# Regrouping the attention matmuls between the halves of a second matrix product

## The chip, the cores and the metric

One core of one Trainium2 chip. The metric is the device time of the whole program in microseconds; most executions agree within 0.3%, so a difference of 2% (5.1 us) counts as faster or slower and anything less as the same class. Differences under 1% were measured in five alternating rounds against the kernel before on the same chip. Every ratio below is the mean time of one kernel's fast runs over that of the other's of the same rounds, so it is not quite the ratio of the medians that stand beside it.

## The reference, cut to what matters

```python
a   = exp(phi - max) / sum(...)                 # softmax over the 576 rows, 32 memory slots
k_m = einsum('bhsm,bhsd->bhmd', a, k)           # 32 x 64 per head
v_m = einsum('bhsm,bhsd->bhmd', a, v)
x   = softmax(q @ k_m.T / 8) @ v_m              # 8 batches, 8 heads, 576 rows, head dim 64
x   = x.transpose(0, 2, 1, 3).reshape(8, 576, 512)
xn  = (x - mean) / sqrt(var + 1e-6) * g_ln
out = x + relu(xn @ w_ch1) @ w_ch2              # 512 -> 2048 -> 512
```

## The kernel before

The kernel folds v and the first weight into W1b (128 x 2048 for each of two groups of heads), so that a batch's first product is `h = W1b^T Eh`, with Eh the normalised attention weights. A batch then has a first product (16 column blocks j, tile h_ps, evicted as relu into rT) and a second one (ch_ps, 16 matmuls for each output tile of 128 rows, done in halves of 8). Two batches hold nine output tiles: even batches do four, odd ones five. Between the halves of batch b's second product TensorE does the attention part of batch b+1:

```python
    def big(shape, dtype, name):                 # three buffers of two PSUM banks
        return psum.tile(shape, dtype, name=name, tag="big", bufs=3)
    def one(shape, dtype, name):                 # two buffers of one bank: ch_ps
        return psum.tile(shape, dtype, name=name, tag="one", bufs=2)
    ...
    for b in range(1, B):
        mm1(b, 0, JC)                            # first product
        ...
        ex[0] += [a_exp(nb), a_qT(nb, 0), a_kv(nb)]      # after half 0 (lambdas, cut)
        ex[1] += [a_tr(nb)]                              # transposes of k and v
        ex[1] += [x_tiles(pr, t1)]                       # attention output, o_ps, and statistics
        ex[2] += [a_sum(nb), a_w1b(nb, 0), a_w1b(nb, 1)] # softmax sums; W1b, two chunks
        ex[3] += [a_sc(nb), a_vb(nb)]                    # scores
        ex[4] += [a_den(nb)]                             # denominators
        ex[6 if odd else 5] += [a_w1b(nb, 2), a_w1b(nb, 3)]
        ex[8 if odd else 6] += [x_tiles(nb // 2, ...)]   # first two tiles of the next batch
        ...
                mm2(pr, t, 8 * half, 8 * (half + 1))     # a finished tile is put out at once
```

In the names below, kv is the product of exp(phi) with k and v, tr the transposes of its result, sc the scores, den the softmax denominators, o the attention output, and vb the masked copy of v that the o matmuls read. The kv, score, W1b and o matmuls use 64-row tiles of the array (`tile_position`); transposes, sums, denominators and both products use all 128 rows. A tile is put out by one VectorE operation, `x = ch_ps * rstd + x`, which frees its ch_ps buffer; rstd comes from VectorE statistics and two small ACT operations, Ln and Exp.

The softmax here doesn't subtract the row's maximum and nothing guards it: scores larger than these inputs give would overflow.

## Time and profile before

| | before |
|---|---|
| median | 257.06 us (256.99 to 257.06, 3 runs) |
| span of the profiled run | 254.5 us |
| busy: TensorE, VectorE, ACT, GpSimd | 95%, 61%, 51%, 20% |
| batch 1 (from 55.31), even, odd, batch 7 | 30.53, 26.20, 30.03, 29.98 us |

The last row is read from the chain of waits, between the starts of the first products; the prediction shows the lines. The profiled execution was timed at 256.29 us, 0.77 under the median.

### The profile page before, as it was taken

What the parts mean: (1) busy time and instruction counts of PE and PEld (TensorE: products, weight loads), DVE (VectorE), ACT (ScalarE), POOL (GpSimd) and SP (SyncE); (2) the same over time, 40 slices, a digit from 0 to 9 for tenths busy, and PEclk for the clock granted to TensorE, in tenths of its full rate; (3) what the DMA queues carried; (4) which work ended last, traced back from release to release, by engine and by line L of the source; (5) the groups of instructions that cost most, each with busy time, mean ns of one, the idle gap of its engine ahead of it and who ended that gap; (6) DMA issues with size and microseconds to landing.
All of it is one profiled execution on the core that took longest, in us unless ns stands there. A gap on an engine that the chain in (4) does not pass through costs nothing.

```text
span 254.5 us, 5778 instructions
## 1 busy us (share of the span) xinstructions
PE 241.0 (95%) x2422; PEld 131.6 (52%) x2453; DVE 155.0 (61%) x306; ACT 129.1 (51%) x219; POOL 51.8 (20%) x87
## 2 busy tenths in 40 slices
PE   7978999899999999999999999999999999999994
PEld 2534555457434665457444664466544764466453
DVE  3346763684486845695486737684568638683431
ACT  3165662668444582648343672558253663565210
POOL 8633330000900009000710018000900022000000
PEclk9999999999999999999999999999999999999999
DMA  7999999999497492988399483969398541130133
GB/s 157 196 207 207 206 255 231 267 183 159 89 208 148 95 213 44 205 174 152 109 173 204 90 195 56 215 140 175 90 202 177 112 76 41 45 78 5 44 82 82
DMA packets 41922, 36.82 MB, mean 145 GB/s; under 512 B 17444, under 2 KB 37160, under 8 KB 41896
## 3 DMA queue, kind: packets, MB, share of 16 engines
q0 software_dynamic: 17248, 19.53, 45.2%
q1 hardware_dynamic: 24488, 16.79, 28.9%
q8 instruction: 19, 0.31, 0.5%
q10 hardware_dynamic: 160, 0.13, 0.2%
q14 instruction: 7, 0.06, 0.1%
HBM read 41.42 MB, written 9.44 MB: 200 GB/s over the span
## 4 chain that ended last, share of the span: by engine, by line
PE 76%; DMA 17%; DVE 3%; issue 2%; ACT 1%; POOL 1%; POOLq 0%
PE ch_ps L438 42%; PE h_ps L374 22%; DMA q_bf<-in_q_dram 7%; DMA w2b<-in_moe_w_ch_dram 6%; DMA kv_bf<-in_k_dram 3%; PE w1b_ps L353 3%; PE o_ps L404 2%; PE kv_ps L205 2%; PE den_ps L327 2%; PE last_ps L450 1%; PE sc_ps L310 1%; DVE bst L416 1%; POOL q_bf L92 1%; DVE w1b L357 1%; ACT x_sb L410 0%
## 5 line engine op out<-in xcount | busy, mean ns | idle before, releaser
L438 PE MATMUL ch_ps<-w2b,rT 128*128 128x512 bf16 x531 | 125.9, 380 | 2.2 <-issue 1.3
L438 PEld LDWEIGHTS <-rT 128*128 128x128 bf16 x560 | 51.3, 98 | 62.3 <-issue 6.7
L374 PE MATMUL h_ps<-Eh,w1b 128*128 128x288 bf16 x512 | 67.1, 285 | 0.7 <-ACT rT L380 0.5
L380 ACT ACTIVATE rT<-h_ps 128x576 bf16<-128x576 f32 x88 | 52.6, 648 | 21.3 <-PE h_ps L374 21.1
L374 PEld LDWEIGHTS <-w1b 128*128 128x128 bf16 x512 | 49.6, 97 | 17.8 <-issue 2.6
L357 DVE SCALAR_TENSOR_TENSOR w1b<-m_sb,rsum,w1b_ps 128x512 bf16<-128x512 f32 x64 | 43.6, 739 | 4.2 <-ACT m_sb L169 2.6
L382 DVE TENSOR_SCALAR rT<-h_ps 128x576 bf16<-128x576 f32 x40 | 30.3, 757 | 24.0 <-PE h_ps L374 23.9
L410 ACT ACTIVATE x_sb<-o_ps 128x1024 f32<-128x1024 f32 (+1 forms) x20 | 18.6, 937 | 37.8 <-PE o_ps L404 36.5
L462 DVE SCALAR_TENSOR_TENSOR x_sb<-ch_ps,rstd,x_sb 128x512 f32<-128x512 f32 x35 | 26.1, 745 | 15.0 <-PE ch_ps L438 14.4
L189 POOL TENSOR_TENSOR es<-e_sb 128x512 f32<-128x512 bf16 x6 | 6.9, 1149 | 137.9 <-ACT e_sb L182 137.9
L416 DVE BATCH_NORM_STATS2 bst<-x_sb 128x6 f32<-128x512 f32 x36 | 24.4, 677 | 8.1 <-ACT x_sb L410 8.1
L339 DVE SCALAR_TENSOR_TENSOR Eh<-E_sb,rs,rden 128x576 bf16<-128x576 bf16 x16 | 12.4, 814 | 14.1 <-ACT rden L338 14.1
L315 ACT ACTIVATE E_sb<-sc_ps,rs 128x640 bf16<-128x640 f32 x16 | 11.9, 790 | 11.6 <-PE sc_ps L310 11.6
L424 ACT ACTIVATE rstd<-mv,eps_sb 128x2 f32<-128x2 f32 (+1 forms) x20 | 5.9, 296 | 20.3 <-DVE mv L417 20.3
L353 PE MATMUL w1b_ps<-w1r,kvT 64*32 64x512 bf16 x256 | 10.8, 383 | 0.8 <-DVE kvT L258 0.4
L227 DVE CAST v<-kv_ps 128x128 bf16<-128x128 f32 x8 | 2.3, 290 | 14.7 <-ACT k L220 13.7
L174 PE MATMUL w_ps<-fill 128*128 128x512 f32 x14 | 9.7, 814 | 1.6 <-DVE fill L119 1.6
L329 ACT ACTIVATE rden<-den_ps 128x576 f32<-128x576 f32 x16 | 9.5, 644 | 2.7 <-PE den_ps L327 2.7
L182 ACT ACTIVATE e_sb<-phi_st 128x1152 bf16<-128x1152 f32 x8 | 9.2, 1151 | 2.7 <-DMA phi_st<-in_phi_dram 2.7
L338 ACT ACTIVATE rden<-rden 128x576 f32<-128x576 f32 x16 | 10.0, 681 | 0.0
L205 PEld LDWEIGHTS <-e_sb 64*32 64x32 bf16 x648 | 6.3, 90 | 5.0 <-ACT e_sb L182 3.0
L92 POOL DMA_DIRECT2D q_bf<-in_q_dram x10 | 7.6, 757 | 4.6 <-DMA w2b<-in_moe_w_ch_dram 1.9
(69 smaller groups left out, 143.6 us busy)
## 6 DMA issues: line engine op xcount, KB each, us to landing
out_dram<-x_sb SPq DMA_DIRECT2D x70, 128.0 KB, 2.5
kv_bf<-in_k_dram POOLq DMA_DIRECT2D x7, 576.0 KB, 7.0
kv_bf<-in_v_dram POOLq DMA_DIRECT2D x7, 576.0 KB, 9.4
phi_st<-in_phi_dram SPq DMA_DIRECT2D x6, 576.0 KB, 4.7
q_bf<-in_q_dram POOLq DMA_DIRECT2D x6, 576.0 KB, 11.9
w1r<-in_moe_w_ch_dram POOLq DMA_DIRECT2D x4, 512.0 KB, 12.9
w2b<-in_moe_w_ch_dram POOLq DMA_DIRECT2D x4, 512.0 KB, 18.9
q_bf<-in_q_dram POOLq DMA_DIRECT2D x4, 288.0 KB, 11.9
```

The costliest lines, as they stand in the source:

```text
L205: nc.tensor.matmul(ps[32 * j:32 * (j + 1), g, 0:D * (sl.stop - sl.start)], e[r:r + TS, c, j, :], kv[r:r + TS, j, sl, D * c:D * (c + 1)], s ...
L315: nc.scalar.activation(out=E_[:, g].rearrange("p (a x) -> p a x", a=2), in_=sc[:, :, 0:HP], func=AF.Exp, scale=s["rs"][:, g:g + 1])
L339: nc.vector.scalar_tensor_tensor(out=Eh[:, g, :], in0=s["E"][:, g, 0:S], scalar=s["rs"][:, g:g + 1], in1=rd[:, g].rearrange("p a x -> p (a ...
L353: nc.tensor.matmul(ps[32 * j:32 * (j + 1), g, :], s["kvT"][r:r + 64, 2, 32 * j:32 * (j + 1)], w1r[r:r + 64, j, fs], start=True, stop=True, ...
L357: nc.vector.scalar_tensor_tensor(out=s["w1b"][:, g, fs], in0=m_sb[:, fs], scalar=s["rsum"][:, g:g + 1], in1=ps[:, g, :], op0=ALU.mult, op1 ...
L374: nc.tensor.matmul(h_ps[:, half, 0:HS], s["w1b"][:, g, P * j:P * (j + 1)], s["Eh"][:, g, HS * half:HS * (half + 1)], start=(g == 0), stop= ...
L380: nc.scalar.activation(out=dst, in_=h_ps[:, :, 0:HS], func=AF.Relu)
L382: nc.vector.tensor_scalar(out=dst, in0=h_ps[:, :, 0:HS], scalar1=0.0, scalar2=None, op0=ALU.max)
L410: nc.scalar.activation(out=x[:, 0:n].rearrange("p i (u y) -> p i u y", u=2), in_=o_ps.rearrange("p u (i y) -> p i u y", i=2)[:, 0:n], func ...
L416: nc.vector.bn_stats(out=stt, in_=x[:, i, :])
L438: nc.tensor.matmul(ch_ps, rT[:, j, P * t:P * (t + 1)], w2b[:, j, :], start=(j == 0), stop=(j == JC - 1))
L462: nc.vector.scalar_tensor_tensor(out=x, in0=ch_ps, scalar=rstd, in1=x, op0=ALU.mult, op1=ALU.add)
```

## The change

Its intent is to give TensorE fewer and longer groups of attention work: sums, kv and four tiles' o_ps in one group; scores with one W1b chunk; three W1b chunks in another. To allow that, exp and the loads move forward into the batch before, statistics are taken apart from `x_tiles`, and the outputs of an even batch's last two tiles (an odd one's last) go inside the next first product. The core of the diff, cuts marked:

```diff
     def a_kv(b):
         ps = big([P, 2, 512], FP32, "kv_ps")
-        kv_mm(b, ps, slice(0, 2))
         if b < 2:
             kv_sum(b, ps)
-            rs_out(b, ps)
-        k_out(b, ps, True)
+        else:
+            for i in range(2):
+                nc.tensor.matmul(ps[:, 0, P:P + 2], st8[b]["es"][:, i, :], ones8, ...)
+        kv_mm(b, ps, slice(0, 2))
+        k_out(b, ps, b < 2)                      # k now copied by VectorE
         v_out(b, ps[:, :, D:2 * D])
+        rs_out(b, ps)
...
-            nc.vector.tensor_tensor(out=vb[:, g], in0=vsl, in1=vmask, op=ALU.mult)
+            eng = nc.vector if b < 2 else nc.gpsimd
+            eng.tensor_tensor(out=vb[:, g], in0=vsl, in1=vmask, op=ALU.mult)
...
+        mm1(b, 0, 4)
+        for f in late[0:1]: f()                  # rstd and an output of the batch before
+        mm1(b, 4, 7)
+        for f in late[1:2]: f()
+        mm1(b, 7, JC)
...
+        half(0); a_kv(nb); x_tiles(pr, t[0:2], False); x_tiles(pr, t[2:4], False)
+        half(1); a_tr(nb); x_stats(pr, t[0]); x_stats(pr, t[1])
+        half(2); a_sc(nb); x_rstd(pr, t[0:2]); a_w1b(nb, 0); mm2_out(pr, t[0])
+        half(3); a_den(nb, finish=False); mm2_out(pr, t[1]); x_stats(pr, t[2])
+        half(4); a_den2(nb)                      # odd: x_tiles(t[4]); even: three W1b chunks
+        half(5); a_exp(nb + 1)                   # odd: mm2_out(pr, t[2])
+        half(6)                                  # odd: three W1b chunks, statistics of t[4]
...                                               # (conditions and the rest cut)
```

More of the change, by code (lines that the diff above doesn't have):

```diff
@@ L179, in a_exp @@
     def a_exp(b):
-        phi_st, kv, q_bf = loaded[b]
+        phi_st, kv, _ = loaded[b]
         e = att.tile([P, NS, 4, M], BF16, name="e_sb")
@@ L183, in a_exp @@
                              in_=phi_st.rearrange("p j (c m) -> p j c m", m=M), func=AF.Exp)
-        st8[b] = {"e": e, "kv": kv, "q": q_bf}
+        st8[b] = {"e": e, "kv": kv}
         if b >= 2:
@@ L236, in a_kv @@
         ps = big([P, 2, 512], FP32, "kv_ps")
-        kv_mm(b, ps, slice(0, 2))
         if b < 2:
             kv_sum(b, ps)
-            rs_out(b, ps)
-        k_out(b, ps, True)
+        else:
+            for i in range(2):
+                nc.tensor.matmul(ps[:, 0, P:P + 2], st8[b]["es"][:, i, :], ones8,
+                                 start=(i == 0), stop=(i == 1))
+        kv_mm(b, ps, slice(0, 2))
+        k_out(b, ps, b < 2)
         v_out(b, ps[:, :, D:2 * D])
+        rs_out(b, ps)
     def a_tr(b, k_part=True, v_part=True):
@@ L263, in a_tr @@
             s["rsum"] = rsum
-    def a_sum(b):
-        ps = big([P, 2, 512], FP32, "sum_ps")
-        for i in range(2):
-            nc.tensor.matmul(ps[:, 0, P:P + 2], st8[b]["es"][:, i, :], ones8,
-                             start=(i == 0), stop=(i == 1))
-        rs_out(b, ps)
     def a_vb(b):
@@ L277, in a_vb @@
             vsl = s["v2"][:, g, :].unsqueeze(1).to_broadcast([P, 4, D])
-            nc.vector.tensor_tensor(out=vb[:, g], in0=vsl, in1=vmask, op=ALU.mult)
+            eng = nc.vector if b < 2 else nc.gpsimd
+            eng.tensor_tensor(out=vb[:, g], in0=vsl, in1=vmask, op=ALU.mult)
         s["vb"] = vb
+    qTs = {}
     def a_qT(b, i):
-        s = st8[b]
+        q_bf = loaded[b][2]
+        if i == 0:
+            qTs[b] = att.tile([P, 4, NP, P], BF16, name="qT")
         if b > 1:
-            if i == 0:
-                s["qT"] = att.tile([P, 4, NP, P], BF16, name="qT")
-                nc.sync.dma_start_transpose(out=s["qT"].rearrange("p j n x -> p (j n) x"),
-                                            in_=s["q"].rearrange("p j n x -> p (j n x)"))
+            nc.sync.dma_start_transpose(out=qTs[b].rearrange("p j n x -> p (j n) x"),
+                                        in_=q_bf.rearrange("p j n x -> p (j n x)"))
             return
-        if i == 0:
-            s["qT"] = att.tile([P, 4, NP, P], BF16, name="qT")
         q_ps = big([P, 2, 1024], BF16, "qT_ps")
@@ L294, in a_qT @@
             for n in range(NP):
-                nc.tensor.transpose(q_ps[:, u, P * n:P * (n + 1)], s["q"][:, 2 * i + u, n, :], ident)
-        dst = s["qT"][:, 2 * i:2 * i + 2].rearrange("p a n x -> p a (n x)")
+                nc.tensor.transpose(q_ps[:, u, P * n:P * (n + 1)], q_bf[:, 2 * i + u, n, :], ident)
+        dst = qTs[b][:, 2 * i:2 * i + 2].rearrange("p a n x -> p a (n x)")
         if i == 0 or b == 1:
@@ L303, in a_sc @@
         s = st8[b]
-        kvT, qT = s["kvT"], s["qT"]
+        kvT, qT = s["kvT"], qTs[b]
         E_ = att.tile([P, 2, 2 * HP], BF16, name="E_sb", bufs=1)
@@ L385, with x_tiles @@
     xs = {}
-    def x_tiles(pr, ts):
+    def x_tiles(pr, ts, stats=True):
         n = len(ts)
@@ L413, in x_tiles, with x_stats @@
         mv = moe.tile([P, 2, 2], FP32, name="mv", bufs=4)
-        for i in range(n):
-            stt = moe.tile([P, 6], FP32, name="bst", bufs=4)
-            nc.vector.bn_stats(out=stt, in_=x[:, i, :])
-            nc.vector.bn_aggr(out=mv[:, i, :], in_=stt)
         for i, t in enumerate(ts):
             xs[(pr, t)] = (x[:, i, :], mv, i, n)
+        if stats:
+            for t in ts:
+                x_stats(pr, t)
+    def x_stats(pr, t):
+        x, mv, i, _ = xs[(pr, t)]
+        stt = moe.tile([P, 6], FP32, name="bst", bufs=4)
+        nc.vector.bn_stats(out=stt, in_=x)
+        nc.vector.bn_aggr(out=mv[:, i, :], in_=stt)
     def x_rstd(pr, ts):
@@ L544 @@
     a_den(1)
+    load(2)
+    a_exp(2)
     mm2(0, 3, 4, 12)
@@ L549 @@
     mm2_out(0, 3)
-    load(2)
+    a_qT(2, 0)
+    late = []
     for b in range(1, B):
-        pr = b // 2
-        mm1(b, 0, JC)
+        pr, nb = b // 2, b + 1
         odd = b % 2
-        tiles = [4, 5, 6, 7, 8] if odd else [0, 1, 2, 3]
-        t1, t2 = tiles[2:4], tiles[4:5]
-        nb = b + 1
-        if b > 1:
-            x_rstd(pr, tiles[0:2])
-        ex = {i: [] for i in range(2 * len(tiles))}
-        if nb < B:
-            ex[0] += [lambda: a_exp(nb), lambda: a_qT(nb, 0), lambda: a_kv(nb)]
-            if nb + 1 < B:
-                ex[0] += [lambda: phis.update({nb + 1: load_phi(nb + 1)})]
-            ex[1] += [lambda: a_tr(nb)]
-        if b == 1:
-            ex[0] += [lambda: x_tiles(0, [4, 5]), lambda: x_rstd(0, [4, 5])]
-        ex[1] += [lambda: x_tiles(pr, t1)]
-        if nb < B:
-            ex[2] += [lambda: a_sum(nb), lambda: a_w1b(nb, 0), lambda: a_w1b(nb, 1)]
-        ex[2] += [lambda: x_rstd(pr, t1)]
-        if nb < B:
-            ex[3] += [lambda: a_sc(nb)]
-        if odd:
-            ex[4] += [lambda: x_tiles(pr, t2), lambda: x_rstd(pr, t2)]
-        if nb < B:
-            ex[3] += [lambda: a_vb(nb)]
-            ex[4] += [lambda: a_den(nb)]
-            ex[6 if odd else 5] += [lambda: a_w1b(nb, 2), lambda: a_w1b(nb, 3)]
-            ex[8 if odd else 6] += [lambda: x_tiles(nb // 2, [4, 5] if nb % 2 else [0, 1])]
-            if nb + 1 < B:
-                ex[7] += [lambda: load(nb + 1)]
-        for i, t in enumerate(tiles):
-            if b == B - 1 and t == tiles[-1]:
-                mm2_last(pr, t)
-                continue
-            for half in range(2):
-                mm2(pr, t, 8 * half, 8 * (half + 1))
-                for f in ex[2 * i + half]:
-                    f()
@@ new lines, with half @@
+        t = [4, 5, 6, 7, 8] if odd else [0, 1, 2, 3]
+        more = nb < B
+        last = not more
+        mm1(b, 0, 4)
+        for f in late[0:1]:
+            f()
+        mm1(b, 4, 7)
+        for f in late[1:2]:
+            f()
+        mm1(b, 7, JC)
+        for f in late[2:]:
+            f()
+        late = []
+        def half(i):
+            if not (last and i >= 8):
+                mm2(pr, t[i // 2], 8 * (i % 2), 8 * (i % 2 + 1), finish=False)
+        half(0)
+        if more:
+            a_kv(nb)
@@ new lines @@
+        x_tiles(pr, t[0:2], False)
+        x_tiles(pr, t[2:4], False)
+        if nb + 1 < B:
+            phis[nb + 1] = load_phi(nb + 1)
+            load(nb + 1)
+        half(1)
+        if more:
+            a_tr(nb)
+        x_stats(pr, t[0])
+        x_stats(pr, t[1])
+        if nb + 1 < B:
+            a_qT(nb + 1, 0)
+        half(2)
+        if more:
+            a_sc(nb)
+        x_rstd(pr, t[0:2])
+        if more:
+            a_w1b(nb, 0)
+        mm2_out(pr, t[0])
+        half(3)
@@ new lines @@
+        if more:
+            a_den(nb, finish=False)
+        mm2_out(pr, t[1])
+        x_stats(pr, t[2])
+        if odd or last:
+            x_stats(pr, t[3])
+            x_rstd(pr, t[2:4])
+        half(4)
+        if more:
+            a_den2(nb)
+        if odd:
+            x_tiles(pr, t[4:5], False)
+        else:
+            a_w1b(nb, 1)
+            a_w1b(nb, 2)
+            a_w1b(nb, 3)
+        if more:
+            a_vb(nb)
+        half(5)
+        if odd or last:
+            mm2_out(pr, t[2])
@@ new lines, with tail @@
+        if nb + 1 < B:
+            a_exp(nb + 1)
+        half(6)
+        if odd:
+            if more:
+                a_w1b(nb, 1)
+                a_w1b(nb, 2)
+                a_w1b(nb, 3)
+            x_stats(pr, t[4])
+            x_rstd(pr, t[4:5])
+        half(7)
+        if odd:
+            mm2_out(pr, t[3])
+            half(8)
+            half(9)
+            if last:
+                mm2_last(pr, t[4])
+            else:
+                late = [lambda pr=pr, tt=t[4]: mm2_out(pr, tt)]
+        else:
+            x_stats(pr, t[3])
+            def tail(pr=pr, tt=t[2:4]):
+                x_rstd(pr, tt)
+                mm2_out(pr, tt[0])
+            late = [tail, lambda pr=pr, tt=t[3]: mm2_out(pr, tt)]
```

## The prediction

> **What bounds the kernel now.** I read the page first (busy shares, then the costliest groups), then a table by stage, then the chain of waits in order of time, then the timeline around the places where the chain leaves TensorE.
>
> ```profile
> PE 241.0 (95%) x2422; PEld 131.6 (52%) x2453; DVE 155.0 (61%) x306; ACT 129.1 (51%) x219; POOL 51.8 (20%) x87
> ```
>
> TensorE is busy 95% of the span, no other engine over 61%. The stage table below, cut at the starts of the first products, shows one even batch (2), one odd batch (3), and batch 4; columns are the stretch, its length, then busy time of PE, PEld, DVE, ACT, POOL, the granted clock, the DMA share and GB/s.
>
> ```profile
> 85.84:112.04 26.20, 25.87 (x275) 14.41 (x278) 17.28 (x34) 14.68 (x25) 6.00 (x10) 1.00 0.81 161
> 112.04:142.08 30.04, 29.59 (x292) 15.99 (x294) 19.97 (x40) 15.67 (x28) 6.00 (x10) 1.00 0.73 142
> 142.08:168.29 26.21, 25.88 (x275) 14.40 (x278) 17.30 (x34) 14.68 (x25) 6.01 (x10) 1.00 0.81 161
> ```
>
> An even batch (four output tiles) takes 26.20 us and an odd one (five) 30.04, and TensorE is busy for all but 0.3 to 0.45 of it. So there is almost no waiting to take away; only TensorE time itself can go. Where that is, the chain of waits shows for batch 4 (start, length, what; some matmul records are missing, so an x7 group and an "issue" beside it are one group of 8):
>
> ```profile
> 142.08 7.96 PE h_ps L374 x64
> ...
> 151.78 0.80 PE kv_ps L205 x72
> ...
> 154.58 0.33 PE o_ps L404 x8
> 154.91 1.83 PE ch_ps L438 x8
> 156.74 0.03 PE sum_ps L269 x2
> 156.77 0.56 PE w1b_ps L353 x16
> ...
> 159.16 0.40 PE sc_ps L310 x16
> 159.56 1.83 PE ch_ps L438 x8
> 161.39 0.49 PE den_ps L327 x4
> 161.88 1.73 PE ch_ps L438 x8
> 163.61 0.56 PE w1b_ps L353 x16
> ...
> 165.99 0.46 PE o_ps L404 x12
> ```
>
> Eight matmuls of the second product take 1.73 us after den_ps (full 128x128 weights) but 1.83 after kv, o, w1b or sc (64-row weights). **So each return from a 64-row group costs 0.10.** Entry costs too: 16 w1b matmuls take 0.56, and one chunk of 8 in the start took 0.34, so a further chunk is 0.22 and some 0.12 is paid once per group. For o_ps, 4, 8 and 12 matmuls take 0.22, 0.33 and 0.46: 0.11 to 0.13 per four, and about 0.10 once.
>
> Batch 1 is the exception, with two true waits in TensorE:
>
> ```profile
> 69.97 0.63 PE L353 MATMUL w1b_ps<-w1r,kvT 64*32 64x512 bf16 x16 [0.41 <-DVE kvT L258]
> 73.13 0.33 PE L310 MATMUL sc_ps<-qT,kvT 64*32 64x320 bf16 x8 [0.44 <-DVE w1b L357]
> ```
>
> **What the Trainium skill says.** "TensorEngine Tiling (Array Packing)", section Key Properties: changing the tiling mode, not just the tile, drains TensorE. The trace agrees, at 0.10 us per return and about 0.1 per entry. "PSUM — Partial Sum Buffer", section on bank collisions: two engines must not read the same bank and quadrant together, so software orders them. Here the v copy on VectorE starts only after ACT's k copy ended (v idle 13.7 us in total until ACT k), so moving k to VectorE makes three copies run back to back and gives no parallelism away. "SBUF — State Buffer", section Who interferes with whom: GpSimd and a VectorE operation with two SBUF inputs exclude one another; that bears on vb on GpSimd. No row before shows it clearly, and I give it nothing below.
>
> **The change, part by part.** (1) *Merged groups.* An even batch now has 64-row groups kv, tr with o, w1b, sc, w1b, o: six returns. Afterwards: sum with kv and both o groups; sc with one w1b chunk; three w1b chunks: three. tr and den are full mode and cost no return. I add up the even batch afterwards, with pieces from the chain: h 7.96; half product 1.74; kv with sum and sixteen o matmuls 0.80+0.03+0.33+0.22=1.38; half 1.83; tr 0.17; half 1.73; sc and a chunk 0.40+0.22=0.62; half 1.83; den 0.49; half 1.73; three chunks 0.56+0.22=0.78; halves 1.83, 1.73, 1.73. Sum 25.55, against 26.20: **0.65 less**. The odd batch keeps one o group of four matmuls by itself: 8.13+1.74+1.48+1.83+0.17+1.73+0.62+1.83+0.49+1.73+0.22+1.83+1.73+0.78+1.83+1.73+1.73 = 29.60, against 30.03: **0.43 less**. (The first o group there has 12 matmuls, hence 1.48.)
>
> (2) *Batch 1.* From 55.31 (its first two h groups are done) to 85.84 it takes 30.53. The same sum with 7.19 of h left is 28.64, so 1.89 less: its exp moves before its first product, statistics no longer stand before the kvT copies on VectorE, and both waits above should go. The phi load it needs is issued at 30.7 and took at most 18.8, so it has landed by about 49.5, before the exp's new place near 53: no new wait on ACT. Batch 7 does not gain: it has two 64-row groups before and after, and takes over 12 o matmuls from batch 6 at 0.11 to 0.13 per four, 0.38 more.
>
> Raw: 3 x 0.65 + 2 x 0.43 + 1.89 - 0.38 = 4.3 us.
>
> (3) *A new wait at the fifth half.* ch_ps has two buffers. The output of the first tile was computed right after its own second half; now it stands after sc and its rstd behind both score exps on ACT, while the fifth half product needs its buffer. Rows of batch 4 give the lengths:
>
> ```profile
> 157.75 0.29 ACT L424 ACTIVATE rstd<-mv,eps_sb 128x2 f32<-128x2 f32 x1 [1.77 <-DVE mv L417]
> 158.07 0.20 ACT L425 ACTIVATE rstd<-rstd 128x2 f32<-128x2 f32 x1
> ...
> 159.49 1.48 ACT L315 ACTIVATE E_sb<-sc_ps,rs 128x640 bf16<-128x640 f32 x2 [1.21 <-PE sc_ps L310]
> ```
>
> From sc's start: 0.40 to the first exp (159.09 to 159.49 in the timeline), 1.45 for both, 0.52 for rstd (Ln to the end of Exp), 0.04, the output 0.75, 0.05 to TensorE: 3.21. TensorE gets there in 0.62+1.83+0.49 = 2.94. VectorE is in time (two statistics done about 1.6 after the kvT copies, w1b's two evictions done about 2.3 after sc's start). **So it stands 0.27 us in each of batches 1 to 6: 1.6 us.**
>
> (4) *Outputs inside the first product.* In h, ACT takes 1.19 for two evictions in each 1.50 (idle 0.31), three in a row at the start. After an even batch, rstd (0.52) now stands before the fifth h eviction. With three h buffers I work out TensorE held about 0.12 in batches 3, 5 and 7: 0.36. One output (0.75) fits into VectorE's 0.74 idle per 1.5 us. Evicting three w1b chunks in a row takes 6 x 0.65 = 3.9 us of VectorE; with the two Eh and the statistics it ends just before the next first product asks for the third buffer: no wait, but little room.
>
> (5) *Loads, transposes, vb.* They start earlier; batches 2 to 7 wait for no load before, so nothing is gained. vb leaves 0.48 us per batch of an idle-rich VectorE.
>
> Sum: 4.3 - 1.6 - 0.36 = 2.35 us less. 257.06 - 2.35 = **254.7 us** (0.9% less); the time is taken to fall as the span does.
>
> **Rivals.** *A, the wait of part 3 does not come* (rstd or the exps end earlier than worked out): the raw 4.3 less 0.36 stays, 253.1. For it: 0.27 is a difference of two sums of some 3 us. Against: four serial steps with measured lengths, and the order on ACT is fixed. *B, VectorE or ACT runs late into the first product after even batches* (three chunks, statistics, rstd, two outputs close together, PSUM in three buffers): 0.5 to 1 us more in three batches, and with the waits of part 3 the gain is gone, 256.5 to 257.5. For it: the little room in part 4, and VectorE falls behind in a busy stretch already (batch 1). Against: its 61% share. *C, the waits and exp of batch 1 move rather than vanish*: 1 us less gained, 255.7. *D, the early loads crowd the outputs and a transposed q comes late*: a stall of some us; against it, each load has about a whole batch (26 us), and lands in 12.
>
> **Range and chances.** A bounds the good side with merged groups up to 0.5 better than my sum: 252.6. B bounds the other: 257.0. Even with no new wait at all the raw 4.3 is 1.7%, under the 5.1 that 2% asks, so faster by over 2% is 0.05; slower by over 2% needs a stall in each batch of over 1 us that I do not see: 0.03.
>
> **What would show it.** Right: even batches near 25.8 and odd ones near 30.0 in the stage table; w1b groups of 24 near 0.78; fewer returns at 1.83; a TensorE wait of 0.2 to 0.4 before ch_ps, ended by VectorE's x_sb (output) row, once in each of six batches; short h waits for rT in three. Wrong: those ch_ps waits missing (A) or over 0.6; h_ps waiting for w1b or rT for over 0.5 per batch (B); waits for qT, q or phi loads (D); groups that merge without becoming shorter, which would void part 1.

## The result, and the profile after

The changed kernel takes **253.18 us** in the median (252.65 to 253.49, 4 runs) against 257.02 (256.9 to 257.06, 4 runs); the ratio is 0.9849, with a 95% interval of 0.9832 to 0.9866. It is 1.5% faster, inside the 2% class, and inside the predicted range.

The busy shares of the page after:

```profile
PE 236.7 (94%) x2422; PEld 133.1 (53%) x2453; DVE 154.9 (62%) x300; ACT 125.3 (50%) x213; POOL 60.0 (24%) x99
```

TensorE does the same 2422 recorded matmuls in 4.3 us less. VectorE stays as it was, ACT falls by 3.8 us (from 129.1), and GpSimd rises by 8.2 (from 51.8), mainly by vb. The stage table after (same columns as in the prediction), for batches 1, 2, 3 and 7:

```profile
55.97:84.79 28.82, 28.27 (x287) 15.60 (x291) 19.85 (x39) 14.57 (x26) 12.10 (x22) 1.00 0.90 161
84.79:110.53 25.74, 25.29 (x272) 14.60 (x274) 17.25 (x32) 13.69 (x22) 5.95 (x11) 1.00 0.80 168
110.53:140.17 29.64, 29.09 (x295) 16.22 (x298) 20.11 (x37) 15.44 (x29) 8.69 (x15) 1.00 0.77 148
...
221.29:251.50 30.21, 26.27 (x182) 15.82 (x182) 13.09 (x23) 10.77 (x22) 0.00 (x0) 1.00 0.28 62
```

Set beside the prediction's own sums (its last two rows worked out from its parts):

| stage | before | predicted | after | gain in the trace |
|---|---|---|---|---|
| batch 1 | 30.53 | 30.53 - 1.89 + 0.27 = 28.91 | 28.82 | 1.71 |
| even, three times | 26.20 | 25.55 + 0.27 = 25.82 | 25.74 | 3 x 0.46 |
| odd 3 and 5 | 30.03 | 29.60 + 0.27 + 0.12 = 29.99 | 29.64 | 2 x 0.39 |
| batch 7 | 29.98 | 29.98 + 0.38 + 0.12 = 30.48 | 30.21 | -0.23 |

The gains add up to 3.64 us; the timed medians differ by 3.84. The two profiled spans differ only by 3.0, because the profiled run after began batch 1's first product 0.66 later (55.97 against 55.31); the experiments come back to that.

The chain of waits of batch 4 after (start, length, what), which answers to the chain in the prediction:

```profile
140.17 7.96 PE h_ps L372 x64
...
149.89 0.73 PE kv_ps L205 x72
150.62 0.55 PE o_ps L402 x16
...
153.17 1.73 PE ch_ps L441 x8
154.90 0.31 PE sc_ps L308 x8
155.21 0.02 issue
155.23 1.48 ACT E_sb L313 x2
156.71 0.19 ACT rstd L427
...
157.16 0.76 DVE x_sb L465
157.92 0.04 issue
157.97 1.89 PE ch_ps L441 x8
159.85 0.77 PE w1b_ps L351 x24
```

Two things are to be seen. The groups are merged and cheaper: kv with sixteen o matmuls takes 0.73 + 0.55 = 1.28, where kv took 0.80 and o groups of 8 and 12 took 0.33 and 0.46 elsewhere; three W1b chunks take 0.77, as worked out (0.78). And the chain now leaves TensorE once in each of batches 1 to 6: from the first scores it runs through both exps on ACT, rstd, and VectorE's output (x_sb), whose end at 157.92 lets the fifth half product start at 157.97. That is the new wait that the prediction named.

### The profile page after: what moved, and what is told of

Its sections match the earlier page's. It is cut to its first block, busy times and chain, and to the rows that moved or that the text cites. A ratio compares the mean times of both kernels' runs of the same rounds, so it can differ in the third digit from the quotient of the medians.

```text
span 251.5 us, 5775 instructions
## 1 busy us (share of the span) xinstructions
PE 236.7 (94%) x2422; PEld 133.1 (53%) x2453; DVE 154.9 (62%) x300; ACT 125.3 (50%) x213; POOL 60.0 (24%) x99
## 4 chain that ended last, share of the span: by engine, by line
PE 72%; DMA 17%; ACT 5%; DVE 2%; issue 2%; POOL 1%; POOLq 0%
PE ch_ps L441 41%; PE h_ps L372 22%; DMA q_bf<-in_q_dram 7%; DMA w2b<-in_moe_w_ch_dram 6%; ACT E_sb L313 4%; DMA kv_bf<-in_k_dram 3%; PE w1b_ps L351 2%; PE o_ps L402 2%; DVE x_sb L465 2%; PE kv_ps L205 2%; PE last_ps L453 1%; PE sc_ps L308 1%; POOL q_bf L92 1%; ACT rstd L428 1%; ACT rstd L427 0%
## 5 line engine op out<-in xcount | busy, mean ns | idle before, releaser
L441 PE MATMUL ch_ps<-w2b,rT 128*128 128x512 bf16 x531 | 123.4, 379 | 3.2 <-issue 1.7
L441 PEld LDWEIGHTS <-rT 128*128 128x128 bf16 x560 | 52.1, 98 | 63.8 <-issue 7.0
L408 ACT ACTIVATE x_sb<-o_ps 128x1024 f32<-128x1024 f32 (+1 forms) x20 | 17.8, 933 | 18.4 <-PE o_ps L402 18.4
L276 POOL TENSOR_TENSOR vb<-v,vmask 128x256 bf16<-128x256 bf16 x12 | 7.7, 662 | 59.4 <-DVE rs L232 59.4
L222 DVE CAST k<-kv_ps 128x256 bf16<-128x256 f32 x7 | 3.0, 424 | 12.5 <-PE kv_ps L205 12.5
L261 DVE COPY kvT<-kvT_ps 128x256 bf16<-128x256 bf16 x8 | 2.3, 292 | 12.5 <-PE kvT_ps L259 11.8
```

Source lines behind the costliest of these rows:

```text
L408: nc.scalar.activation(out=x[:, 0:n].rearrange("p i (u y) -> p i u y", u=2), in_=o_ps.rearrange("p u (i y) -> p i u y", i=2)[:, 0:n], func ...
L441: nc.tensor.matmul(ch_ps, rT[:, j, P * t:P * (t + 1)], w2b[:, j, :], start=(j == 0), stop=(j == JC - 1))
```

## The experiments

All are small edits of the changed kernel unless it says otherwise; all gave correct results. Runs of one call shared a chip and the runs of the kernel before. The changed kernel ran in another call, so a difference from it is one of medians across calls; the median of the kernel before was 257.02 to 257.06 in each of them.

**1. rstd ahead of the score exps.**

```diff
-            a_sc(nb)
-        x_rstd(pr, t[0:2])
-        if more:
+        x_rstd(pr, t[0:2])
+        if more:
+            a_sc(nb)
             a_w1b(nb, 0)
```

> The rstd of the first two tiles moves ahead of the two score exps on ACT; nothing else. Theory (the wait at the fifth half product comes from rstd standing behind both exps): the profile of the changed kernel has 0.30 us there in each of six batches. With rstd first the output of the first tile is held only by w1b's two evictions and ends about 0.27 earlier, but the exps start about 0.7 later and the second den product may wait 0.1: 0.17 to 0.27 less per batch, 1.0 to 1.6 us less than the changed kernel (about 251.6 to 252.2). Rival (the wait only moves to den or to VectorE): within 0.3 us of the changed kernel.

It took 251.8 us (251.64 to 252.13, 4 runs; before 257.04; ratio 0.9794, 0.9778 to 0.9811), 1.4 us less than the changed kernel. Its stage table has batch 4 at 25.50 instead of 25.74 (0.24 less; six times that is 1.44). The theory holds: the wait was real, and it came from the order on ACT. Against the kernel before this version lies on the 2% line: 2.06% faster, with an interval of 1.89% to 2.22%, so that by the rule of this page it is unclear whether it counts as faster.

**2. One merge undone: the second o group behind the transposes.**

```diff
         x_tiles(pr, t[0:2], False)
-        x_tiles(pr, t[2:4], False)
...
             a_tr(nb)
+        x_tiles(pr, t[2:4], False)
```

> Undoes one merge: the second o group goes back behind the transposes of kvT, one half product later. Theory (a 64-row group by itself pays about 0.1 us on entry and 0.10 on return): 0.20 us more in each of batches 1 to 7, 1.4 us slower than the changed kernel, with one more half product of 1.83 instead of 1.73 in each batch. Rival (the gain came from the moved statistics and outputs on VectorE, not from fewer groups): no more than 0.3 us slower.

254.76 us (254.48 to 255.17, 6 runs; ratio 0.9912, 0.9897 to 0.9927): 1.58 us slower than the changed kernel, against 1.4 expected. The chain of batch 4:

```profile
150.99 0.33 PE o_ps L402 x8
...
153.32 0.33 PE o_ps L402 x8
153.65 1.83 PE ch_ps L441 x8
```

The two o groups take 0.33 each instead of 0.55 together (0.11 for the extra entry), and the half product behind the second takes 1.83, where it took 1.73 in the changed kernel (0.10 for the extra return). The batch takes 25.95 instead of 25.74. Grouping itself is worth 0.21 us per group saved; the rival, that the moved statistics did it, falls for this part.

**3. A second merge undone: three W1b chunks as one and two.**

```diff
-            a_w1b(nb, 1); a_w1b(nb, 2); a_w1b(nb, 3)     # in one place
+            a_w1b(nb, 1)
+        half(5)                                          # odd: chunk 1 after half 5, the rest after half 6
+            a_w1b(nb, 2); a_w1b(nb, 3)
```

> Undoes the other merge: the three w1b chunks are taken as one and two, with a half product between them, in batches 1 to 6. Theory (0.2 us per extra 64-row group): 1.2 to 1.3 us slower than the changed kernel, w1b groups of 8 and 16 instead of 24 in the chain. Rival (grouping of w1b is free, only the place matters): within 0.3 us; if the later evictions of chunks two and three hold up the next first product, more than 1.5 us slower, with waits of h_ps for w1b.

254.6 us (254.39 to 256.91, 6 runs; ratio 0.9917, 0.9889 to 0.9945): 1.42 slower, against 1.2 to 1.3 expected. The chain of batch 4:

```profile
160.47 0.34 PE w1b_ps L351 x8
160.81 1.83 PE ch_ps L441 x8
162.64 0.56 PE w1b_ps L351 x16
```

0.34 + 0.56 = 0.90 instead of 0.77, and one more half product at 1.83; the batch takes 25.96 (0.22 more). Both merges thus have the same price per group. The third merge of the change, scores with a W1b chunk, was not undone by itself.

**4. Late outputs ahead of the first product instead of inside it.**

```diff
-        mm1(b, 0, 4)
-        for f in late[0:1]: f()
-        mm1(b, 4, 7)
-        for f in late[1:2]: f()
-        mm1(b, 7, JC)
+        for f in late: f()
+        mm1(b, 0, JC)
```

> The late rstd and outputs go ahead of the next first product on ACT and VectorE instead of inside it. Theory (they fit in either place, since ACT and VectorE have time before the first evictions of h, and the changed kernel shows no wait of h_ps in batches 2 to 7): within 0.3 us of the changed kernel. Rival (their place inside the product is what removes the 0.17 us that odd batches' first product lost before): 0.2 to 0.5 us slower per odd batch, 0.6 to 1.5 us in all, with h_ps x24 and a wait for rT in the chain.

253.25 us (252.75 to 253.42, 4 runs; ratio 0.9846), the same as the changed kernel. Its chain has h in one piece of 7.96 us in batches 2 to 7 too. So the place of these outputs inside the product brings nothing; what helps the first product of odd batches is that two statistics no longer stand there, as experiment 7 shows.

**5. k and vb back on their old engines.**

```diff
-        k_out(b, ps, b < 2)
+        k_out(b, ps, True)
...
-            eng = nc.vector if b < 2 else nc.gpsimd
+            eng = nc.vector
```

> k copied by ACT again and vb made by VectorE again, as before the change; all else as changed. Theory (neither lies on TensorE's path: the copies end over a us before the transposes need them, vb is used a batch later): within 0.3 us of the changed kernel; v starts after ACT's k again. Rival (VectorE's place matters: 0.5 us of vb in front of the w1b evictions of each batch, or ACT's k in front of the o copies): 0.2 to 0.5 us per batch, 1 to 3 us slower.

253.07 us (252.83 to 253.47, 4 runs; ratio 0.9842). No difference, though vb takes 661 ns on GpSimd and 285 on VectorE: neither copy lies on TensorE's path. This part of the change is neutral.

**6. The exp of batch 2 back behind batch 1's first product.**

```diff
     load(2)
-    a_exp(2)
...
+        if b == 1:                # after mm1(b, 7, JC)
+            a_exp(2)
```

> The exp of batch 2's phi goes back behind batch 1's first product; the loads stay early. The sum now stands first in the kv group, so TensorE must wait there for exp (1.15), then six GpSimd steps (3.9 with their gaps). Theory (the early exp is what the merged sum needs): the group would start 1.7 us after the first product and has its sums about 5.3 us after it, so about 3.5 us slower than the changed kernel, all of it in batch 1, with a wait of kv_ps on GpSimd in the trace. Rival (the gain in batch 1 comes from the grouping and the statistics alone; the place of exp does not matter): within 0.5 us.

259.15 us (258.42 to 260.17, 6 runs; ratio 1.0075): 5.97 us slower than the changed kernel, against 3.5 expected. The wait came as worked out (first the timeline line of the sums, with the idle time and its releaser in brackets), but more came with it (then the stage table around it; the last three numbers of a row are the granted clock, the DMA share and GB/s):

```profile
68.16 0.19 PE L242 MATMUL kv_ps<-ones,hl 128*128 128x2 bf16 x1 [3.03 <-POOL hl L195]
68.66 0.19 PE L242 MATMUL kv_ps<-ones,hl 128*128 128x2 bf16 x1 [0.32 <-POOL hl L196]
```

```profile
65.20:68.60 3.40, 0.19 (x1) 0.11 (x1) 0.00 (x0) 0.00 (x0) 3.02 (x6) 0.90 0.23 83
68.60:71.40 2.80, 2.40 (x94) 1.89 (x96) 0.70 (x3) 0.72 (x1) 2.72 (x6) 0.50 0.38 39
71.40:74.70 3.30, 3.30 (x10) 1.38 (x10) 0.00 (x0) 1.21 (x2) 1.13 (x2) 0.50 1.20 206
74.70:76.60 1.90, 1.90 (x18) 0.77 (x24) 1.65 (x6) 0.00 (x0) 0.00 (x0) 0.99 1.22 207
```

TensorE waited 3.03 + 0.32 = 3.35 us for GpSimd. Finer windows of the same trace show the granted clock fall to 0.50 at about 67.9, before the first of the two small matmuls, and return at about 74.7. Batch 1 took 35.13 us instead of 28.82, 6.31 more. Of this, 3.70 lies before kv (the wait and the two small matmuls), and 2.61 is work that ran at the half clock: kv 1.09 instead of 0.73, o 1.12 instead of 0.68, the half product 3.52 instead of 1.83 (the piece of seven recorded matmuls and the issue before it), the transposes 0.29 instead of 0.17. The theory holds for the wait, and its size was off because I had not counted the clock. The six executions list mean clocks of 0.987 (the profiled one, 259.85 us, and one of 260.17) and 0.993 (four, 258.42 to 259.61), so the clock's share may differ between them. The Trainium skill has this ("TensorE: Matmul & The Clock Gate", Part 1: The HAM clock gate): after about 3.4 us without work the array falls to half its clock, and needs about as long at work to come back. The trace agrees on the half clock but not on the two times: the clock fell about 2.8 us after the last matmul ended (65.1, a modelled end) and came back about 6.0 us after work began again (68.7). The lesson for the change: the early exp is no detail but what the merged sum group stands on.

**7. The kernel before, with two statistics moved into the first product.** In batches 3, 5 and 7:

```diff
-        mm1(b, 0, JC)
+        mm1(b, 0, 4)
+        x_stats(pr, 4)            # no longer done right after x_tiles in the batch before
+        mm1(b, 4, 7)
+        x_stats(pr, 5)
+        mm1(b, 7, JC)
```

> The kernel before, with one edit: in batches 3, 5 and 7 the statistics of the first two x tiles move from ahead of the first product into it, behind its fourth and seventh eviction. Theory (the 0.17 us that the first product of odd batches loses before, and not after the change, comes from VectorE doing statistics and an output while the fourth h tile waits for eviction): the first product of these batches falls from 8.15 to about 7.96 us, one unbroken group of 64 in the chain; 0.5 us in all, so 256.5. Rival (the loss comes from ACT or from w1b's evictions): h stays broken into 24 and 40 with 8.1 us, and the time stays at 257.0.

256.38 us (255.93 to 256.79, 6 runs) against 257.02; ratio 0.9976, 0.9959 to 0.9994. In the chain of the kernel before, batch 3's first product is broken in two, with a short gap:

```profile
112.04 2.96 PE h_ps L374 x24
115.03 5.15 PE h_ps L374 x40
```

and with the edit it is one piece, 7.96 us:

```profile
112.19 7.96 PE h_ps L374 x64
```

The reason stands in the timeline before: VectorE finished two statistics and an output first, so that its eviction of the fourth h tile began late, 2.19 us after the first product (114.23 against 112.04); with the edit it begins 2.00 after (114.19 against 112.19).

```profile
113.60 0.72 DVE L462 SCALAR_TENSOR_TENSOR x_sb<-ch_ps,rstd,x_sb 128x512 f32<-128x512 f32 x1
114.23 0.75 DVE L382 TENSOR_SCALAR rT<-h_ps 128x576 bf16<-128x576 f32 x1
```

So 0.17 us in each of three batches was a wait of the kernel before, which the change removed by taking those statistics elsewhere.

**8. First statistics, rstd and first output all earlier.**

```diff
+        x_stats(pr, t[0])
         half(1)
         if more:
             a_tr(nb)
-        x_stats(pr, t[0])
         x_stats(pr, t[1])
...
-            a_sc(nb)
         x_rstd(pr, t[0:2])
+        mm2_out(pr, t[0])
         if more:
+            a_sc(nb)
             a_w1b(nb, 0)
-        mm2_out(pr, t[0])
```

> The changed kernel with the first tile's statistics ahead of the kvT copies on VectorE (idle there for 1.8 us), and rstd and the first output ahead of the scores. Theory: rstd then starts about 0.8 us earlier than with rstd moved alone, so that neither the fifth half product waits for ch_ps (0.30) nor the second den product for its exp (0.22 with rstd moved alone): an even batch of 25.3 us against 25.74, 0.45 less in six batches, 2.4 to 2.8 us less than the changed kernel, 250.4 to 250.8. Rival (something else then holds TensorE, such as w1b's evictions 0.4 later): no better than 251.8.

251.69 us (251.5 to 251.9, 4 runs; before 257.06; ratio 0.9787, 0.9774 to 0.9801): as good as experiment 1 and no better than the rival's 251.8, so my number was missed. Its stage table:

```profile
84.53:109.98 25.45, 25.13 (x272) 14.62 (x274) 17.24 (x32) 13.76 (x22) 5.54 (x10) 1.00 0.82 170
109.98:139.33 29.35, 28.93 (x295) 16.26 (x298) 20.35 (x38) 15.52 (x29) 9.13 (x16) 1.00 0.77 151
```

The error was in reading experiment 1. There the chain gives den 0.71, and I took 0.22 of it for a wait; but the half product before it shows only seven matmul records, and the missing eighth (0.16) is counted with den. The wait was 0.06, and that is about what this version gains (25.45 against 25.50). With it no wait for ch_ps is left, so 25.74 - 25.45 = 29.64 - 29.35 = **0.29 us** is what the new wait costs the changed kernel per batch. The rest of an even batch is nearly all TensorE work (25.13 of 25.45 us are recorded as busy, and some matmul records are missing).

**9. The kernel before once more.** A copy without edits, one look.

> The kernel before once more, for one more profile of its start. The changed kernel and its variants begin the long stretch of batch 1's first product 0.4 to 0.9 us later than the one profile of before (55.7 to 56.3 against 55.31). Theory: that is the scatter of the loads at the start between executions, so this profile lies anywhere from 55.3 to 56.3. Rival: the changed order delays the last q load, so before lies at 55.3 again.

One run, of unknown state, 256.73 us. Batch 1's long stretch of the first product began at 55.67. The three profiles with the old order thus give 55.31, 55.45 (experiment 7) and 55.67; the eight with the new order 55.53 to 56.26. The two overlap, but the old order's mean is 0.4 lower. The spans settle most of it. From that start to the end a kernel takes nearly the same time in every profile: 199.19 and 199.23 us in the two of the kernel before, 195.53 and 195.52 in those of the changed kernel and of experiment 4. So the starts of the unprofiled runs can be estimated from their spans: 11 runs of the kernel before have a median span of 255.2, which puts the start at about 56.0; the four of the changed kernel have 251.4, which puts it at about 55.9. The early starts came with profiled executions faster than the medians (256.29, 255.93 and 256.73), and by this estimate the new order of loads costs nothing that shows.

## Why the prediction was right or wrong

The time was within the range. The mechanism was right in parts 1, 2, 3 and 5 and wrong in part 4; the gain was 3.84 us instead of 2.35. The time by itself would have misled: 253.18 is what rival A forecast (253.1), yet A's mechanism, that the wait of part 3 does not come, is false. The wait came, and other gains happened to make up for it. Of the 1.49 between them, 1.30 shows in the stage table: 2 x 0.35 in batches 3 and 5, 0.27 in batch 7, 3 x 0.08 in the even ones and 0.09 in batch 1. The other 0.2 us is the difference between timed runs and trace; the early start of the profiled execution before (experiment 9) accounts for most of it, by estimate.

- **Part 1, merged groups: right.** Entry and return were put at about 0.1 each; undoing a merge cost 0.21 and 0.22 per batch. The sum for kv with o was 0.07 too high (1.38 with the sums' 0.03; measured 1.31), because kv itself is shorter (0.73 instead of 0.80) when a group of the same kind follows it. That is most of the 0.08 in even batches. In the odd ones its pieces add up to 1.51, not 1.48; measured were 0.03 + 0.73 + 0.68 = 1.44.
- **Part 2, batch 1: right in size** (28.91 predicted, 28.82 measured; the sum is 0.02 short, as 29.60 - 8.13 + 7.19 is 28.66), and batch 7's extra o work too (0.38 predicted; 0.23 more in all after 0.17 less of h, so 0.40). That exp had to be early was shown by experiment 6. How the 1.71 us splits between grouping and the moved statistics was not tried separately.
- **Part 3, the new wait for ch_ps: right**, 0.27 predicted and 0.29 measured in both kinds of batch, and shown by two versions that take it away. Both of its sums were a little long, and the errors nearly cancel: from the start of sc to the fifth half product the trace after has 3.14 us (154.83 to 157.97) where 3.21 was worked out, and TensorE without the wait gets there in 2.84 (experiment 8, 153.98 to 156.82), not 2.94. Rival A, that it would not come, fell.
- **Part 4, "I work out TensorE held about 0.12 in batches 3, 5 and 7": wrong, and the largest error.** h takes 7.96 us in each of batches 2 to 7 after the change: nothing is held, and the short h waits that the prediction listed as a sign are missing. My ACT sum, which the prediction does not show, took its evictions at about 0.6 each. In the trace rstd follows the three evictions in a row (1.73), and the fifth tile's eviction starts 2.58 us after the first product in batch 5 against 2.49 in batch 4, which has no rstd there: 0.09 late, yet the product takes 7.96 in both. What is more, the sum for odd batches carried over their 8.13 of first product as if it were work. It held a wait of 0.17 (experiment 7), which the change removed. Together that is 0.29 us in each of three batches, 0.87 of the 1.30.
- **Part 5: right.** Loads and transposes cost no wait, and vb and k are neutral (experiment 5).
- **Rivals B, C and D fell**: no first product waits in batches 2 to 7, batch 1 gained in full, and no load or transposed q shows up in the waits of TensorE after the start.

## What to carry to other kernels

Where an engine is full, ask what each switch between kinds of work costs, and gather work of one kind; here each group saved was worth 0.2 us. When work is moved together, follow the buffer that it frees: the merged order put an output behind two exps and gave back 0.29 us per batch, and one moved line won 1.4 us of it. And when two stages of the same work have different lengths (7.96 and 8.13), the longer one can hide a wait: look for it before carrying it into a sum.

## What the Trainium skill lacked or had wrong

- "TensorEngine Tiling (Array Packing)", Key Properties, says that changing the tiling mode drains TensorE, and gives no figure. Here one more 64-row group among 128-row work costs 0.21 to 0.22 us, 0.11 to 0.13 in the group and 0.10 in the half product after it (that a drain is the cause, the runs do not show); 128-row work in between (den_ps, the transposes) costs no return: the half product behind it takes 1.73.
- "TensorE: Matmul & The Clock Gate", Part 1, gives about 3.4 us both for the idle time before the half clock and for the work before the full one. In the one profile of experiment 6 the clock fell after about 2.8 us without a matmul and came back after about 6.0 us of work; the half clock cost 2.61 us on top of the wait of 3.35.
- "SBUF — State Buffer", Who interferes with whom, warns of GpSimd and VectorE shutting each other out. Moving vb to GpSimd (661 ns against 285), together with k to VectorE, changed the time by 0.1 us, but it was no test of the lock: VectorE stood idle all through vb in each of the six batches (in batch 4 from 151.37 to 153.21, with vb from 151.45 to 152.74). No run here shows the lock.
